# Two-layer sliding-window transformer on one core: row maxima that write two SBUF buffers in turn, and probability-times-value blocks ordered by key half

## The chip, the cores and the metric

The program runs on one core of one Trainium2 chip. The metric is the device time of the whole program in microseconds (us), the median of several runs. The names of the engines are those of the profile: PE (TensorE; PEld are its weight loads), DVE (VectorE), ACT (ScalarE), POOL (GpSimd) and SP (SyncE, which issues most DMAs).

## The reference

Two layers of attention (A) and feed-forward (B), with the same weights in both. 2048 rows of 640 numbers, 32 heads of 20, a causal window of 256 keys, a hidden width of 1536:

```python
scores = jnp.einsum("bhqd,bhkd->bhqk", q, k) * (Dh ** -0.5)
mask = (idx[:, None] - idx[None, :] >= 0) & (idx[:, None] - idx[None, :] < W)      # W = 256
scores = jnp.where(mask[None, None], scores, -1e9)
p = _softmax(scores, axis=-1)
o = jnp.einsum("bhqk,bhkd->bhqd", p, v)
...
x = x + _A_ref(_layernorm(x, axis=-1), A_wqkv, A_wo)
x = x + _B_ref(_layernorm(x, axis=-1), B_w1, B_b1, B_w2, B_b2)    # relu(h)^2 between w1 and w2
x = x + _A_ref(...)
x = x + _B_ref(...)
```

## The kernel before

The rows are cut into 16 **units** (8 groups of 256 rows in each of 2 layers, `u` = 0 to 15). A unit's attention is done in 8 **quads** of 4 heads. Because a row sees itself and 255 rows before it, a unit reads the keys of its own group (two blocks of 128, `kb` 2 and 3) and of the group before (`kb` 0 and 1). Units 0 and 8, the first groups of the layers, have only `kb` 2 and 3. That leaves 14 units, or 112 quads, with four blocks.

For one quad the work goes in five steps:

- `max_quad`: PE computes the scores once with queries on the partitions into `five`, five banks of PSUM (line 568; line 615 in units 0 and 8). DVE then takes the row maxima with eight `tensor_tensor_reduce` (`reduce`, line 578). Each adds a mask and writes the masked scores back over `five`, and is two instructions on DVE: the reduction (CUSTOM_DVE_ANT_0) and the read of its accumulator into `mx` (DVE_READ_ACCUMULATOR2_ANT).
- `max_out`: every second quad, the maxima are transposed (line 633), negated and sent by DMA into spare rows of `qt`, so that the next matmul subtracts them.
- `exp_quad`: PE computes the scores again with keys on the partitions, minus the maxima (line 684, line 693 in units 0, 1 and 8), into the same `five` and a further bank `sixth`. It has to wait until DVE has read the maxima out of `five`. ACT takes the exponentials into SBUF tiles `pt` (line 707). POOL sets what lies outside the window to zero (lines 722 and 726). Six exponentials and eight masks belong to a quad, in three steps: `kb` 1; `kb` 0 and 3; `kb` 2.
- `pv_quad`: PE multiplies by the values (line 765). The array is used as eight tiles of 64 rows by 32 columns: two **key halves** (`h`, the upper and the lower 64 keys of a block) times four heads. Half 0 sums in `pv`, half 1 in `sixth`. Since a half of an edge block sees only part of the queries, a block streams 256 and 192, or 128 and 64, columns in its two halves. The numbers are float32, so that each matmul shows as two records; a quad has 32 matmuls and 64 records here, and is called a **burst** below.
- ACT and DVE copy and add the two halves (lines 795 and 803), and DMA takes them away.

All the dense matmuls (projections and feed-forward, line 263, in float16 pairs) are poured between these steps by hand: `together` runs `exp_quad(n)`, some dense work, `max_quad` of a quad nine further on, `pv_quad(n)`, some dense work. The order on every engine is that in which the Python code emits it (a manual schedule). DVE, ACT and POOL jobs are queued with modelled costs and are emitted when the model says that they can start; `need` moves the model's clock on. `by_tiles` sorts the matmuls of a burst by where each would start in its own tile's stream, and `steps_of` lists the blocks of each step.

Of the kernel before, what the change touches and what calls it, by code (L numbers as in the profile page):

```python
# [12 lines left out]
BF16 = mybir.dt.bfloat16  # L13
AF = mybir.ActivationFunctionType
ALU = mybir.AluOpType

P = 128
Q = P // 2
# [27 lines left out]
def kernel(ctx: ExitStack, tc: tile.TileContext, x, wqkv, wo, w1, b1, w2, b2, out):  # L46
# [12 lines left out]
    maskb = sb.tile([P, 3 * P], BF16, name="maskb")  # L59
    nc.vector.memset(maskb, 0.0)  # L60

    nc.gpsimd.affine_select(out=maskb, in_=maskb, pattern=[[1, 3 * P]], compare_op=ALU.is_gt,
                            fill=NEG, base=0, channel_multiplier=-1)
    nc.gpsimd.affine_select(out=maskb, in_=maskb, pattern=[[-1, 3 * P]], compare_op=ALU.is_ge,
                            fill=NEG, base=2 * P, channel_multiplier=1)
    maskq = sb.tile([P, 5 * Q], BF16, name="maskq")
    b1s = sb.tile([P, FC], F32, name="b1s")
    kts = []
    for i in range(3):
# [469 lines left out]
    def by_tiles(pieces):  # L539
# [11 lines left out]
    maskj = []  # L551

    def max_pieces(n, e, w, x0, x1, m):

# [20 lines left out]

    def reduce(v, mask, accum, cols):

        bbjobs.append(post("D", 113 + 1.047 * cols, lambda: nc.vector.tensor_tensor_reduce(  # L578
            out=v, in0=v, in1=mask, scale=1.0, scalar=-3.0e38, op0=ALU.add, op1=ALU.max, accum_out=accum),
            prio=urgency["turn"]))  # L580

    def max_quad(n):

        u, qd = divmod(n, NQ)
        qt, cur = qts[u], kts[u % 3]
        G = qd // GQ
        if (u, G) not in mxs:
            mxs[u, G] = sb.tile([P, 2, 2 * GQ, 2], F32, name="mx", bufs=2)
        mx = mxs[u, G]
        need(trips[u, 0, qd], trips[u, 1, qd])  # L590
        banks()
        accum = {(e, w): mx[:, e, (2 * qd + w // 2) % (2 * GQ), w % 2:w % 2 + 1] for e in range(2) for w in range(4)}
        if u % NG:
            if not maskj:
                maskj.extend(post("D", 250, lambda h=h: nc.vector.tensor_copy(
                    maskq[h * Q:(h + 1) * Q, :], maskb[h * Q:(h + 1) * Q, h * Q:(h + 5) * Q]), prio=0) for h in range(2))
            need(*maskj)
            by_tiles([x for e in range(2) for w in TURN[e]
                      for x in max_pieces(n, e, w, LATER if w == 0 else 0, 5 * Q, Q)])
            now[0] += 656.0  # L600

            def rest():
                by_tiles([x for e in range(2) for x in max_pieces(n, e, 0, 0, LATER, P // 4)])
                now[0] += 110.0
# [5 lines left out]
            return  # L610
        for w in range(4):
            j, i = divmod(w, 2)
            for e in range(2):
                r, n_, o = slice(64 * e, 64 * e + 3 * DH), (i + 1) * P, i * P
                nc.tensor.matmul(five[:, 3 * e + j, o:o + n_], qt[r, 2 * qd + j, i * P:(i + 1) * P],
                                 cur[r, 2 * qd + j, :n_], start=True, stop=True)
        now[0] += 440.0
        for w in range(4):
            j, i = divmod(w, 2)
            for e in range(2):  # L620
                o, n_ = i * P, (i + 1) * P
                reduce(five[:, 3 * e + j, o:o + n_], maskb[:, 3 * P - n_:], accum[e, w], n_)
        mxjobs[u, G] = list(bbjobs)

    mxjobs = {}
# [109 lines left out]
    def steps_of(u):  # L735

        cur, prev = kts[u % 3], kts[(u - 1) % 3]
        if u % NG == 0:
            return [[(2, cur, 0, 0, 2)], [(3, cur, P, 1, 1)]]
        return [[(1, prev, P, 0, 2)], [(0, prev, 0, 0, 1), (3, cur, P, 1, 1)], [(2, cur, 0, 0, 2)]]  # L740

    def pv_quad(n, quad):
        u, qd = divmod(n, NQ)
        steps = steps_of(u)
        while rest_of:
            rest_of.pop()()
        pv, jobs = mm_tile([P, T], "pv")
        if u % NG:
            last_bank()
            two = (pv, sixth[:, :T])  # L750
            for k, pts in enumerate(quad[0]):
                need(*quad[1][k])
                pieces = []
                for kb, kt, ko, q0, qn in steps[k]:
                    vf = vts[(2 * (u if kb >= 2 else u - 1) + kb % 2) % 6][1]
                    for h in range(2):
                        a, b = seen(kb, h, qn * P)
                        for e, kb_, _, _, box, part in pts:
                            for j in range(2 if kb_ == kb else 0):
                                jj = 2 * j + e  # L760
                                c = (4 * qd + jj) * (DH + 1)

                                def put(h=h, kb=kb, jj=jj, c=c, j=j, vf=vf, box=box, part=part, a=a, b=b, q0=q0, k=k):
                                    pj = box["pt"][h * Q:(h + 1) * Q, part].rearrange("p (j n) -> p j n", j=2)
                                    nc.tensor.matmul(two[h][32 * jj:32 * (jj + 1), q0 * P + a:q0 * P + b],  # L765
                                                     vf[h * Q:(h + 1) * Q, c:c + 32], pj[:, j, a:b], start=(kb == 1),
                                                     stop=(k == len(steps) - 1), skip_group_check=True,
                                                     tile_position=(h * Q, 32 * jj))

                                pieces.append(((h, jj), b - a, put))  # L770
                by_tiles(pieces)
                now[0] += 410.0
        for k, pts in enumerate([] if u % NG else quad[0]):
            need(*quad[1][k])
            for kb, kt, ko, q0, qn in steps[k]:
                vf = vts[(2 * (u if kb >= 2 else u - 1) + kb % 2) % 6][1]
                for j in range(2):
                    for e, kb_, _, _, box, part in pts:
                        if kb_ == kb:
                            jj = 2 * j + e  # L780
                            c = (4 * qd + jj) * (DH + 1)
                            pj = box["pt"][:, part].rearrange("p (j n) -> p j n", j=2)
                            nc.tensor.matmul(pv[32 * jj:32 * (jj + 1), q0 * P:(q0 + qn) * P],
                                             vf[:, c:c + 32], pj[:, j, :], start=(k == 0),
                                             stop=(k == len(steps) - 1), skip_group_check=True,
                                             tile_position=(0, 32 * jj))
            now[0] += 480.0 if u % NG else 400.0
        if qd == 0:
            ods[u] = tc.dram_tile([DH + 1, H, T], F32, name=f"o{u}")
        if qd % 2 == 0:  # L790
            ots[u] = sb.tile([P, 2, T], F32, name="ot", bufs=2)
        ot = ots[u]

        def out():
            nc.scalar.copy(ot[:, qd % 2], pv)  # L795

        def write():
            drv = ods[u].rearrange("d (q j) n -> j d q n", j=4)
            for j in range(4):
                nc.sync.dma_start(drv[j][:, qd - 1:qd + 1, :], ot[32 * j:32 * j + DH + 1])  # L800

        def add():
            nc.vector.tensor_tensor(ot[:, qd % 2], ot[:, qd % 2], sixth[:, :T], op=ALU.add)  # L803
# [403 lines left out]
```

## Time and profile before

| | |
|---|---|
| median of 3 runs | 1659.91 us (1655.34 to 1662.32) |
| profiled execution: time | 1655.08 us |
| profiled execution: span of the trace | 1653.4 us |
| TensorE clock granted, mean | 0.994 |
| busy: PE, PEld | 1574.8 us (95%), 1209.9 us (73%) |
| busy: DVE, ACT, POOL | 1091.6 us (66%), 734.2 us (44%), 620.9 us (38%) |
| row maxima on DVE, 128 x 320 each (line 578) | 896 reductions, mean 497 ns |
| accumulator reads (line 578) | 1024, mean 141 ns |
| chain that ended last | PE 69%, DVE 18%, ACT 4% |

An instruction's row has its start, its length, its engine, its line in the kernel, what it writes and reads, and its shape; in brackets stands how long its engine was idle before it and what ended that. A matmul's length includes its way through the array, so that matmuls in a row overlap and only their starts tell the pace.

### The profile page before, as it was taken

What the parts mean: (1) busy time and instruction counts of PE and PEld (TensorE: products, weight loads), DVE (VectorE), ACT (ScalarE), POOL (GpSimd) and SP (SyncE); (2) the same over time, 40 slices, a digit from 0 to 9 for tenths busy, and PEclk for the clock granted to TensorE, in tenths of its full rate; (3) what the DMA queues carried; (4) which work ended last, traced back from release to release, by engine and by line L of the source; (5) the groups of instructions that cost most, each with busy time, mean ns of one, the idle gap of its engine ahead of it and who ended that gap; (6) DMA issues with size and microseconds to landing.
All of it is one profiled execution on the core that took longest, in us unless ns stands there. A gap on an engine that the chain in (4) does not pass through costs nothing.

```text
span 1653.4 us, 61438 instructions
## 1 busy us (share of the span) xinstructions
PE 1574.8 (95%) x25926; PEld 1209.9 (73%) x25926; DVE 1091.6 (66%) x3364; ACT 734.2 (44%) x1593; POOL 620.9 (38%) x1288
## 2 busy tenths in 40 slices
PE   8888999999999999999999999999999999998899
PEld 6666777777777777777777777777777777676667
DVE  8876766676757667576566767567675766857441
ACT  4454544445453444534443453534535444453422
POOL 1222534435342443524323352533534344353412
PEclk9999999999999999999999999999999999999999
DMA  9755244243433524343352435335253352421020
GB/s 267 186 138 138 51 111 93 64 124 67 118 79 98 122 51 117 82 119 85 86 130 56 113 86 122 79 93 110 62 120 86 102 102 59 105 67 54 27 64 17
DMA packets 234283, 159.16 MB, mean 96 GB/s; under 512 B 82200, under 2 KB 217752, under 8 KB 234008
## 3 DMA queue, kind: packets, MB, share of 16 engines
q1 hardware_dynamic: 227640, 145.74, 36.7%
q10 hardware_dynamic: 6368, 9.50, 2.0%
q8 instruction: 203, 3.33, 0.9%
q14 instruction: 72, 0.59, 0.1%
HBM read 84.68 MB, written 52.95 MB: 83 GB/s over the span
## 4 chain that ended last, share of the span: by engine, by line
PE 69%; DVE 18%; ACT 4%; issue 3%; POOL 3%; DMA 2%; SPq 0%; DVEq 0%; ACTq 0%; POOLq 0%
PE acc L263 51%; DVE five L578 10%; PE pv L765 5%; PE five L684 4%; PE five L568 4%; DVE mx L578 2%; ACT pt L707 2%; PE sixth L765 2%; POOL pt L726 2%; DVE hh L972 1%; DVE ot L803 1%; ACT r L962 1%; PE tr L633 1%; PE five L693 1%; DMA o<-ot 1%
## 5 line engine op out<-in xcount | busy, mean ns | idle before, releaser
L578 DVE CUSTOM_DVE_ANT_0 five<-five,maskq 128x320 f32<-128x320 f32 x896 | 445.6, 497 | 105.9 <-PE five L568 84.1
L707 ACT ACTIVATE pt<-five 128x512 f32<-128x512 f32 (+1 forms) x624 | 319.1, 595 | 267.5 <-PE sixth L684 216.3
L722 POOL TENSOR_SCALAR_AFFINE_SELECT pt<-pt 128x256 f32<-128x256 f32 x448 | 203.0, 462 | 545.6 <-ACT pt L707 528.1
L263 PE MATMUL acc<-y,w_s 128*128 128x256 f16 x2880 | 330.7, 273 | 5.3 <-ACT y L312 2.1
L263 PE MATMUL acc<-w_s,hh 128*128 128x320 f16 x2304 | 326.7, 299 | 0.0
L263 PEld LDWEIGHTS <-w_s 128*128 128x128 f16 x2880 | 277.9, 98 | 53.8 <-issue 19.4
L263 PEld LDWEIGHTS <-hh 128*128 128x128 f16 x2304 | 221.8, 98 | 94.2 <-issue 9.9
L726 POOL TENSOR_SCALAR_AFFINE_SELECT pt<-pt 128x256 f32<-128x256 f32 x512 | 227.5, 466 | 102.2 <-ACT pt L707 94.5
L263 PE MATMUL acc<-yT,wq_s 128*128 128x256 f16 x2250 | 260.0, 274 | 5.0 <-DVE qd L440 2.4
L263 PEld LDWEIGHTS <-wq_s 128*128 128x128 f16 x2400 | 231.4, 98 | 45.0 <-issue 12.9
L972 DVE TENSOR_TENSOR hh<-r,hh 128x256 f16<-128x256 f32 x192 | 90.9, 504 | 180.0 <-ACT hh L969 175.7
L966 POOL TENSOR_TENSOR r<-r 128x256 f32<-128x256 f32 x192 | 114.0, 614 | 185.6 <-ACT r L962 184.0
L765 PE MATMUL pv<-pt,vt 64*32 64x256 f32 (+3 forms) x3584 | 169.2, 301 | 5.1 <-DVE x L900 2.9
L765 PE MATMUL sixth<-pt,vt 64*32 64x192 f32 (+3 forms) x3584 | 159.7, 302 | 1.7 <-issue 1.7
L795 ACT COPY ot<-pv 128x256 f32<-128x256 f32 x128 | 47.6, 372 | 249.6 <-PE sixth L765 168.5
L263 PE MATMUL acc<-wo_s,od 128*128 128x320 f16 x960 | 141.1, 301 | 4.3 <-DVE od L876 2.9
L578 DVE DVE_READ_ACCUMULATOR2_ANT mx<- 128x1 f32 x1024 | 144.5, 141 | 0.0
L263 PE MATMUL acc<-wq_s,yT 128*128 128x320 f16 x900 | 134.1, 302 | 4.0 <-DVE y L313 2.8
L962 ACT ACTIVATE r<-acc,b1s 128x256 f32<-128x256 f32 x192 | 80.6, 471 | 107.9 <-PE acc L263 107.8
L263 PEld LDWEIGHTS <-od 128*128 128x128 f16 x960 | 91.6, 98 | 47.8 <-issue 5.0
L263 PEld LDWEIGHTS <-yT 128*128 128x128 f16 x900 | 87.2, 99 | 41.3 <-issue 9.9
L765 PEld LDWEIGHTS pv<-pt,vt 64*32 64x32 f32 x3584 | 101.3, 106 | 18.8 <-POOL pt L726 8.8
(96 smaller groups left out, 1617.4 us busy)
## 6 DMA issues: line engine op xcount, KB each, us to landing
qt<-qk SPq DMA_DIRECT2D x30, 480.0 KB
kt<-qk SPq DMA_DIRECT2D x30, 480.0 KB
qk<-qd SPq DMA_DIRECT2D x17, 640.0 KB
o<-ot SPq DMA_DIRECT2D x256, 42.0 KB
od<-o SPq DMA_DIRECT2D x14, 640.0 KB
qk<-yl SPq DMA_DIRECT2D x13, 640.0 KB
qk<-qd SPq DMA_DIRECT2D x17, 320.0 KB
xt<-in_A_x_dram SPq DMA_DIRECT2D x16, 320.0 KB
```

Source lines behind the costliest of these rows:

```text
L263: nc.tensor.matmul(acc, lhs(a, c), rhs(b, c), start=(k == 0), stop=(k == 3 * nk - 1))
L568: nc.tensor.matmul(flat[t * m:(t + 1) * m, o:o + b - a], qt[r, p, i * P + t * m:i * P + (t + 1) * m], kt[r, p, a + to:b + to], start=True, ...
L578: bbjobs.append(post("D", 113 + 1.047 * cols, lambda: nc.vector.tensor_tensor_reduce(out=v, in0=v, in1=mask, scale=1.0, scalar=-3.0e38, op ...
L684: nc.tensor.matmul(sbank[e][k][rows, o + a:o + b], kt[r, 2 * qd + j, ko + 64 * h:ko + 64 * (h + 1)], qt[r, 2 * qd + j, q0 * P + a:q0 * P + ...
L707: nc.scalar.activation(box["pt"][:, :o], sbank[e][k][:, :o], AF.Exp, scale=SCALE / (QS * QS))
L722: nc.gpsimd.affine_select(out=m, in_=m, pattern=[[0, 2], [-1, P]], compare_op=ALU.is_gt, fill=0.0, base=0, channel_multiplier=1)
L726: nc.gpsimd.affine_select(out=m, in_=m, pattern=[[0, 2], [1, P]], compare_op=ALU.is_ge, fill=0.0, base=0, channel_multiplier=-1)
L765: nc.tensor.matmul(two[h][32 * jj:32 * (jj + 1), q0 * P + a:q0 * P + b], vf[h * Q:(h + 1) * Q, c:c + 32], pj[:, j, a:b], start=(kb == 1), ...
L795: nc.scalar.copy(ot[:, qd % 2], pv)
L962: nc.scalar.activation(box["r"], acc[:, f, :], AF.Relu, bias=b1s[:, f0 + f:f0 + f + 1], scale=1.0 / (YS * WS))
L966: nc.gpsimd.tensor_tensor(box["r"], box["r"], box["r"], op=ALU.mult)
L972: nc.vector.tensor_sub(hh[:, 1, f, :], box["r"], hh[:, 0, f, :])
```

## The change

- The row maxima write their elementwise output (which nobody reads) to two bfloat16 buffers in SBUF, `junk0` and `junk1`, in turn, instead of back over `five`.
- The three steps of a quad are now `kb` 1; `kb` 2; `kb` 3 and 0. `pv_quad` takes the first two together and then the third, and each half goes through the blocks in an order of its own (`AFTER`), so that both halves stream 256, 192, 128, 64 columns, in that order. The first matmul of a sum (`start`) and the last (`stop`) follow this order.
- The masks of the maxima are packed: `maskq` alone, and a small `maskz`. They are built by POOL at the start, in place of two DVE copies made before their first use. So that they fit units 0 and 8 too, the scores there (line 615 before, 626 after) are computed in 64-query halves: 20 matmuls in a quad in place of 8.

```diff
+    masks = sb.tile([P, 3 * P], BF16, name="pt", tag="pt", bufs=6)
+    maskq = sb.tile([P, 5 * Q], BF16, name="maskq")
+    maskz = sb.tile([P, P], BF16, name="maskz")
...
+    nc.gpsimd.affine_select(out=maskz, in_=maskz, pattern=[[-1, P]], compare_op=ALU.is_ge,
+                            fill=NEG, base=0, channel_multiplier=1)
+    for h in range(2):
+        nc.gpsimd.tensor_copy(maskq[h * Q:(h + 1) * Q, :], masks[h * Q:(h + 1) * Q, h * Q:(h + 5) * Q])
...
+    junk, junked = [sb.tile([P, 5 * Q], BF16, name=f"junk{i}") for i in range(2)], []
...
     def reduce(v, mask, accum, cols):
-        bbjobs.append(post("D", 113 + 1.047 * cols, lambda: nc.vector.tensor_tensor_reduce(
-            out=v, in0=v, in1=mask, scale=1.0, scalar=-3.0e38, op0=ALU.add, op1=ALU.max, accum_out=accum),
-            prio=urgency["turn"]))
+        j = junk[len(junked) % 2]
+        junked.append(0)
+
+        def put():
+            nc.vector.tensor_tensor_reduce(out=j[:, :cols], in0=v, in1=mask, scale=1.0, scalar=-3.0e38,
+                                           op0=ALU.add, op1=ALU.max, accum_out=accum)
+
+        bbjobs.append(post("D", 113 + 1.047 * cols, put, prio=urgency["turn"]))
...
-            if not maskj:
-                maskj.extend(post("D", 250, lambda h=h: nc.vector.tensor_copy(
-                    maskq[h * Q:(h + 1) * Q, :], maskb[h * Q:(h + 1) * Q, h * Q:(h + 5) * Q]), prio=0) for h in range(2))
-            need(*maskj)
...
-                nc.tensor.matmul(five[:, 3 * e + j, o:o + n_], qt[r, 2 * qd + j, i * P:(i + 1) * P],
-                                 cur[r, 2 * qd + j, :n_], start=True, stop=True)
+                for h in range(2):
+                    for o, n_ in ([(0, P)] if i == 0 else [(P, 4 * Q)] if h else [(P, Q), (P + Q, 3 * Q)]):
+                        def put(e=e, r=r, p=p, h=h, i=i, j=j, o=o, n_=n_):
+                            nc.tensor.matmul(five[h * Q:(h + 1) * Q, 3 * e + j, o:o + n_], ...)
...
+    AFTER = ((2, 1, 3, 0), (1, 2, 0, 3))
...
-        return [[(1, prev, P, 0, 2)], [(0, prev, 0, 0, 1), (3, cur, P, 1, 1)], [(2, cur, 0, 0, 2)]]
+        return [[(1, prev, P, 0, 2)], [(2, cur, 0, 0, 2)], [(3, cur, P, 1, 1), (0, prev, 0, 0, 1)]]
...
-            for k, pts in enumerate(quad[0]):
-                need(*quad[1][k])
+            for ks, ns in (((0, 1), 830.0), ((2,), 400.0)):
+                need(*[j for k in ks for j in quad[1][k]])
...
-                    for h in range(2):
+                for h in range(2):
+                    for k, kb, kt, ko, q0, qn in sorted(blocks, key=lambda t: AFTER[h].index(t[1])):
...
-                                                     vf[h * Q:(h + 1) * Q, c:c + 32], pj[:, j, a:b], start=(kb == 1),
-                                                     stop=(k == len(steps) - 1), skip_group_check=True,
+                                                     vf[h * Q:(h + 1) * Q, c:c + 32], pj[:, j, a:b],
+                                                     start=(kb == 2 - h), stop=(kb == 3 * h), skip_group_check=True,
```

What this does to the order on two engines is shown here; the rows have the line, the operation and the tiles, and in brackets the engines whose semaphores an instruction waits for.

The first place is DVE, in a quad in the middle of a unit with four blocks. Before, three reductions with their accumulator reads and then the addition of the two halves (line 803) stand there:

```order
L578 ISA five,mx<-five,maskq 128x320 [waits PE_49]
L578 ISA mx 128x1
L578 ISA five,mx<-five,maskq 128x320 [waits DVE_49]
L578 ISA mx 128x1
L803 TENSOR_TENSOR ot<-ot,sixth 128x256 [waits DMAHW6_49,DMAHW0_49,DMAHW7_49,PE_49,Activation_49]
```

And after the change (the reduction is now on line 588):

```order
L588 ISA junk_135,mx<-five,maskq 128x320 [waits PE_49]
L588 ISA mx 128x1
L588 ISA junk_136,mx<-five,maskq 128x320
L588 ISA mx 128x1
L588 ISA junk_135,mx<-five,maskq 128x320 [waits DVE_49]
L588 ISA mx 128x1
L823 TENSOR_TENSOR ot<-ot,sixth 128x256 [waits DMAHW6_49,DMAHW0_49,DMAHW7_49,PE_49,Activation_49]
```

Nothing has changed its place. The second reduction waited for the first and waits for nothing now; the third still waits for DVE itself, because it writes the buffer that the one two places ahead wrote.

The second place is PE, one burst with the dense matmul behind it; `vt` with a number is the values of one block, `x4` are the four heads, and the last number is the columns streamed. Before:

```order
L765 MATMUL pv<-pt,vt_90 32x192 x4
L765 MATMUL sixth<-pt,vt_90 32x256 x4
L765 MATMUL pv<-pt,vt_87 32x64 x4
L765 MATMUL sixth<-pt,vt_87 32x128 x4
L765 MATMUL pv<-pt,vt_96 32x128 x4
L765 MATMUL sixth<-pt,vt_96 32x64 x4
L765 MATMUL pv<-pt,vt_93 32x256 x4
L765 MATMUL sixth<-pt,vt_93 32x192 x4
L263 MATMUL acc<-yT,wq_s 128x256
```

After (now on lines 785 and 269):

```order
L785 MATMUL pv<-pt,vt_100 32x256 x4
L785 MATMUL sixth<-pt,vt_97 32x256 x4
L785 MATMUL pv<-pt,vt_97 32x192 x4
L785 MATMUL sixth<-pt,vt_100 32x192 x4
L785 MATMUL pv<-pt,vt_103 32x128 x4
L785 MATMUL sixth<-pt,vt_94 32x128 x4
L785 MATMUL pv<-pt,vt_94 32x64 x4
L785 MATMUL sixth<-pt,vt_103 32x64 x4
L269 MATMUL acc<-yT,wq_s 128x256
```

The same 32 matmuls stand in the burst, 640 columns in each half; each pair of rows now has equal lengths. How much dense work stands between the steps on PE is the same in nearly all units.

More of the change, by code (lines that the diff above doesn't have):

```diff
@@ L620, in max_quad @@
             for e in range(2):
-                o, n_ = i * P, (i + 1) * P
-                reduce(five[:, 3 * e + j, o:o + n_], maskb[:, 3 * P - n_:], accum[e, w], n_)
+                if i:
+                    reduce(five[:, 3 * e + j, P:3 * P], maskq[:, Q:], accum[e, w], 2 * P)
+                else:
+                    reduce(five[:, 3 * e + j, :P], maskz, accum[e, w], P)
         mxjobs[u, G] = list(bbjobs)
@@ L750, in pv_quad @@
             two = (pv, sixth[:, :T])
-            for k, pts in enumerate(quad[0]):
-                need(*quad[1][k])
+            for ks, ns in (((0, 1), 830.0), ((2,), 400.0)):
+                need(*[j for k in ks for j in quad[1][k]])
+                blocks = [(k, *block) for k in ks for block in steps[k]]
                 pieces = []
-                for kb, kt, ko, q0, qn in steps[k]:
-                    vf = vts[(2 * (u if kb >= 2 else u - 1) + kb % 2) % 6][1]
-                    for h in range(2):
+                for h in range(2):
+                    for k, kb, kt, ko, q0, qn in sorted(blocks, key=lambda t: AFTER[h].index(t[1])):
                         a, b = seen(kb, h, qn * P)
-                        for e, kb_, _, _, box, part in pts:
+                        vf = vts[(2 * (u if kb >= 2 else u - 1) + kb % 2) % 6][1]
+                        for e, kb_, _, _, box, part in quad[0][k]:
                             for j in range(2 if kb_ == kb else 0):
```

22 lines of the change are left out of this document (13 added, 9 removed).

## The prediction

> **What bounds the kernel now.** I read the page first, then PE's waits in three stretches of the span, then the timelines of DVE and PE around one quad. The page's parts 1 and 4:
>
> ```profile
> PE 1574.8 (95%) x25926; PEld 1209.9 (73%) x25926; DVE 1091.6 (66%) x3364; ACT 734.2 (44%) x1593; POOL 620.9 (38%) x1288
> PE 69%; DVE 18%; ACT 4%; issue 3%; POOL 3%; DMA 2%; SPq 0%; DVEq 0%; ACTq 0%; POOLq 0%
> ```
>
> PE is idle for only 1653.4 − 1574.8 = 78.6 us. So time can be gained in two ways: PE waits less, or its own stream gets shorter. The chain nevertheless runs over DVE for 18%, so the idle time that there is should be DVE's doing. PE's waits (total, times, longest), first from 235 to 1420 us, then from 1420 to 1580 us, then from 0 to 235 us:
>
> ```profile
> PE five L684 <- DVE mx L578: 16.3, 23, 1.0
> ```
> ```profile
> PE five L684 <- DVE mx L578: 10.9, 10, 2.1
> PE acc L263 <- DVE od L876: 2.9, 2, 2.5
> ```
> ```profile
> PE five L693 <- DVE mx L578: 6.9, 9, 1.3
> PE pv L765 <- DVE x L900: 2.9, 1, 2.9
> PE acc L263 <- DVE y L313: 2.8, 2, 2.3
> PE five L684 <- DVE mx L578: 1.2, 1, 1.2
> ```
>
> PE wants to overwrite `five` with the second scores (684, 693) while DVE is still taking maxima out of it. That is 16.3 + 10.9 + 6.9 + 1.2 = 35.3 us in 43 waits. In the long middle no wait is over 1.0 us.
>
> **The reductions: how much earlier DVE is done.** DVE's timeline in the quad ahead of one such wait:
>
> ```profile
> 751.81 0.49 DVE L578 CUSTOM_DVE_ANT_0 five<-five,maskq 128x320 f32<-128x320 f32 x1
> ...
> 752.40 0.50 DVE L578 CUSTOM_DVE_ANT_0 five<-five,maskq 128x320 f32<-128x320 f32 x1
> ...
> 752.99 0.50 DVE L578 CUSTOM_DVE_ANT_0 five<-five,maskq 128x320 f32<-128x320 f32 x1
> ...
> 753.40 0.42 DVE L803 TENSOR_TENSOR ot<-ot,sixth 128x256 f32<-128x256 f32 x1
> ...
> 755.07 0.49 DVE L578 CUSTOM_DVE_ANT_0 five<-five,maskq 128x320 f32<-128x320 f32 x1
> ...
> 755.66 0.50 DVE L578 CUSTOM_DVE_ANT_0 five<-five,maskq 128x320 f32<-128x320 f32 x1
> ...
> 756.25 0.50 DVE L578 CUSTOM_DVE_ANT_0 five<-five,maskq 128x320 f32<-128x320 f32 x1
> ...
> 756.84 0.50 DVE L578 CUSTOM_DVE_ANT_0 five<-five,maskq 128x320 f32<-128x320 f32 x1
> ...
> 757.43 0.50 DVE L578 CUSTOM_DVE_ANT_0 five<-five,maskq 128x320 f32<-128x320 f32 x1
> ...
> 757.85 0.69 DVE L440 SCALAR_TENSOR_TENSOR yl<-acc,yl 128x512 f16<-128x512 f32 x1
> ```
>
> Start to start, a reduction that is followed by another takes 0.59 us (755.07 to 755.66, and so on). One that is followed by something else takes 0.41 (752.99 to 753.40) or 0.42 us (757.43 to 757.85). The length, 0.50 us, is the same. The difference is the wait in the order: the next reduction waits for the one before, while the addition and the line 440 do not. The accumulator read lies between in both cases and costs nothing in the second.
>
> With two buffers, the remaining wait is for the reduction two places ahead. That one started 2 × 0.415 = 0.83 us ago and took 0.50, so the wait is over before it is asked for. I therefore expect 0.415 us also between reductions, a gain of 0.175 us a pair. Not shown by this trace is a reduction started right behind an accumulator read without a wait, nor one that writes SBUF. The far bound is no gain at all (0.59). I take 0.415, since all the followers without a wait stand there, among them line 440, which reads PSUM and writes SBUF; a gain beyond it has no row. The quad above has six such pairs, so its last maximum comes 6 × 0.175 = 1.05 us earlier.
>
> A rule speaks against this: the Trainium skill, "VectorE: DVE Perf Modes", section "The DRAIN you can't avoid", says that after every operation the pipe has to run empty, and that eight copies took as long with a semaphore after each as with one at the end. By it this term would be nothing; the same section says that an operation that is not held starts earlier, and the trace, with 0.41 beside 0.59 us, sides with that half.
>
> **What that is worth on PE.** The wait behind this quad, and a place where PE goes from dense work to the second scores without one:
>
> ```profile
> 740.28 4.75 PE L263 MATMUL acc<-wo_s,od 128*128 128x320 f16 x33
> 744.96 0.63 PE L684 MATMUL five<-qt,kt 62*64 62x192 f16 x23
> ...
> 758.04 0.61 PE L684 MATMUL five<-qt,kt 62*64 62x192 f16 x23 [0.95 <-DVE mx L578]
> ```
>
> - 235 to 1420 us: the longest wait is 1.0 us and the quad comes 1.05 us earlier, so all 16.3 us go.
> - 1420 to 1580 us: ten waits, 1.09 us on average. Less dense work lies between the steps and other DVE work stands between the reductions, so I count 3 to 6 pairs ahead of each, 0.5 to 1.05 us. With what a wait has as its cap I take 7.8 of 10.9 us.
> - 0 to 235 us: ten waits, 8.1 us, nearly all shorter than 1.05 us. I take 7.6 us.
> - The other DVE waits (2.9 + 2.9 + 2.8 us) have 3 to 5 pairs ahead of them in DVE's queue, 0.5 to 0.9 us each; I take 3 us with the smaller ones.
> - Without a wait, PE starts the second scores 0.07 us before the modelled end of the dense matmul (744.96 against 740.28 + 4.75 = 745.03), with one it starts later by the whole idle time. So the waits that go, some 42, bring another 42 × 0.07 = 2.9 us.
>
> Together 16.3 + 7.8 + 7.6 + 3 + 2.9 = 37.6 us. What is late next at these places: nothing that the trace shows. The exponentials, masks and the burst follow the second scores at the same distance as before, and move forward with them.
>
> **The bursts.** PE's timeline of the burst in the same quad:
>
> ```profile
> 750.51 0.88 PE L568 MATMUL five<-kt,qt 60*64 60x64 f16 x45
> 751.21 0.34 PE L765 MATMUL pv<-pt,vt 64*32 64x192 f32 x4
> 751.23 0.39 PE L765 MATMUL sixth<-pt,vt 64*32 64x256 f32 x4
> 751.38 0.33 PE L765 MATMUL pv<-pt,vt 64*32 64x192 f32 x4
> 751.45 0.39 PE L765 MATMUL sixth<-pt,vt 64*32 64x256 f32 x4
> ...
> 752.19 0.41 PE L765 MATMUL pv<-pt,vt 64*32 64x256 f32 x3
> ...
> 752.55 4.54 PE L263 MATMUL acc<-yT,wq_s 128*128 128x256 f16 x40
> ```
>
> Each matmul goes through twice. 192 columns take 751.38 − 751.21 = 0.17 us and 256 take 0.22 us a pass, 0.86 ns a column. A half streams 640 columns twice: 640 × 2 × 0.86 ns = 1.10 us. The last pass of 256 starts at 752.19 and so ends at 752.41 to 752.45; the dense matmul starts 0.12 us later. The least that a burst can take is 1.10 + 0.12 = 1.22 us. It takes 752.55 − 751.21 = 1.34 us, because one half is ahead of the other and the array's weight loads come in order. With equal lengths side by side I expect 1.22 us, 0.12 us less. The bounds are 0 and 0.16 us. Busy time of line 765 in the whole span, and in this burst:
>
> ```profile
> 0.00:1654.00 1654.00, 171.07 (x7168) 122.37 (x7168) 0.99 0.40 96
> ```
> ```profile
> 751.00:753.00 2.00, 1.40 (x64) 1.07 (x64) 1.00 0.72 136
> ```
>
> 7168 / 64 = 112 bursts; the mean, 1.53 us, is not far above this one's 1.40, so most look like it. 112 × 0.12 = 13 us. The merged first group now waits for four masks where it waited for two; that is covered, as POOL shows for the same quad:
>
> ```profile
> 749.03 1.70 POOL L726 TENSOR_SCALAR_AFFINE_SELECT pt<-pt 128x256 f32<-128x256 f32 x3
> 750.71 0.54 POOL L300 TENSOR_TENSOR bmv<-bmv,neghalf 128x1 f32<-128x1 f32 x1
> ...
> 761.65 1.12 POOL L726 TENSOR_SCALAR_AFFINE_SELECT pt<-pt 128x256 f32<-128x256 f32 x3
> ```
>
> All eight masks end at 750.73, 0.48 us before the burst. The third group, which now has four masks in place of two, starts some 0.77 us (2 × 448 columns) into it, so its cover is 1.25 us. In bursts that do wait for the last mask, less work stands behind it than before.
>
> **Small edits.** In units 0 and 8 a quad's first scores are 20 matmuls in place of 8:
>
> ```profile
> 788.40 0.50 PE L615 MATMUL five<-kt,qt 60*128 60x128 f16 x8
> 788.84 0.37 PE L765 MATMUL pv<-pt,vt 64*32 64x192 f32 x4
> ```
>
> The eight take 0.44 us until the burst starts. The streams of the tiles keep their length, and in the row of 45 above a matmul costs 0.70 / 45 = 16 ns; 12 more are between 0 and 0.2 us a quad. For 16 quads I take 16 × 0.1 = 1.6 us. At the start POOL gets a selection and two copies, bounded by three times 0.51 us, ahead of the layernorm's power:
>
> ```profile
> 1.90 0.51 POOL L64 TENSOR_SCALAR_AFFINE_SELECT maskb<-maskb 128x384 bf16<-128x384 bf16 x1
> 5.49 0.55 POOL L300 TENSOR_TENSOR bmv<-bmv,neghalf 128x1 f32<-128x1 f32 x1 [3.09 <-DVE bmv L294]
> ```
>
> It was idle for 3.09 us there, so this costs nothing; without that cover, 1.5 us once.
>
> **The sum.** −37.6 (waits) − 13 (bursts) + 1.6 = −49 us, against the profiled execution's 1655.1 us: 1606.1 us. That execution was 4.8 us below the median of the three runs (1659.9), and as fast as the fastest of them. I take half of that, 2.4 us, as the median's distance: 1608.5 us, 3% less. A measurement of this kernel can tell about 0.5%, 8 us, from no change.
>
> **The rivals.**
> - *The reductions keep their pace.* The accumulator read has to end before the next reduction starts, or the remaining wait binds. Against it stand the 0.41 us followers; for it, that none of them is a reduction. All of the 37.6 us stay: 1608.5 + 37.6 = 1646 us.
> - *The bursts do not get shorter*, since weight loads and not unequal lengths make the 0.12 us. The reductions' part holds: 1608.5 + 13 = 1621.5 us.
> - *Slower: masks late behind reductions that write SBUF.* POOL's three masks took 1.70 us where a DVE operation from SBUF to SBUF ran beside them, and 1.12 us elsewhere (the two rows above), 0.58 us more. If reductions that write SBUF held POOL up like that, the four last masks of each burst would come later. It decides where they are over 1.25 us late, and from 0.44 us of waiting in each of the 112 bursts (49 us) the gain is gone. At 0.6 us each it is 112 × 0.6 = 67 us: 1608.5 + 67 = 1676 us. Against it: in this quad the masks end 1.1 us before the first reduction starts (750.73, 751.81), and a reduction reads a mask from SBUF already.
>
> **How the numbers follow.** Chances: forecast 0.74, unchanged bursts 0.09, unchanged reductions 0.09, late masks 0.08. The bound for faster lies near 1649 us, just above the 1646 us of the unchanged reductions, of which I count two thirds as faster. Faster 0.74 + 0.09 + 0.06 = 0.89, same 0.03, slower 0.08. The range: down to 1592, where the DVE waits left over (9 us) and bursts 0.16 us shorter (4.5 us) go too and the median lies at the profile; up to 1632, where half of the reductions' gain is missing (19 us) and the median lies 4.8 us above the profile. It takes in the unchanged bursts and leaves out the last two cases.
>
> **What would show it.** Right: reductions start every 0.41 to 0.42 us in a row; the waits of 684 and 693 (after: 703 and 712) for the maxima fall from 35 us to about 4; a clean burst takes some 1.22 us to the next dense matmul; PE's idle share falls to about 2.5%, with no new releaser among its waits. Wrong: starts 0.5 us or more apart; bursts that wait for POOL's masks; or PE waiting for ACT or a DMA at the second scores.

## The result, and the profile after

The changed kernel takes 1621.69 us (median of 5, 1619.97 to 1623.61) against 1658.33 us for the kernel before, measured beside it (5 runs). The ratio is 0.978, 95% interval 0.976 to 0.980: 2.2% less. The forecast was 1608.5 us with a range of 1592 to 1632 us; the time lies in it, 13 us above the forecast, where the rival "the bursts do not get shorter" had put it (1621.5 us).

The profiled execution took 1620.96 us (span 1618.9), 34.1 us less than that of before. First the busy row of the page:

```profile
PE 1568.2 (97%) x26118; PEld 1224.5 (76%) x26118; DVE 999.8 (62%) x3363; ACT 734.1 (45%) x1593; POOL 625.3 (39%) x1291
```

PE is idle for 1618.9 − 1568.2 = 50.7 us, where it was 78.6; its busy time fell by 6.6 us. PE's waits over the whole span (total, times, longest):

```profile
PE five L703 <- DVE mx L588: 6.7, 9, 1.4
PE five L574 <- ACT pt L726: 3.1, 5, 1.5
...
PE tr L650 <- DVE yl L446: 2.5, 12, 0.4
...
PE five L712 <- DVE mx L588: 0.6, 2, 0.4
```

The waits for the maxima have fallen from 35.3 us in 43 to 7.3 us in 11. None of them lies between 235 and 1390 us; in the same stretch of work before (235 to 1420 us) there had been 16.3 us. The third row is a wait that hardly showed before (0.4 us, once): the transpose of the maxima (line 650) comes 12 times some 0.2 us too early for DVE. PE's idle share is 3.1%, where the prediction named about 2.5%. DVE's timeline, three reductions in a row with their accumulator reads:

```profile
88.48 0.48 DVE L588 CUSTOM_DVE_ANT_0 junk<-five,maskq 128x320 bf16<-128x320 f32 x1
88.89 0.08 DVE L588 DVE_READ_ACCUMULATOR2_ANT mx<- 128x1 f32 x1
88.89 0.48 DVE L588 CUSTOM_DVE_ANT_0 junk<-five,maskq 128x320 bf16<-128x320 f32 x1
89.30 0.08 DVE L588 DVE_READ_ACCUMULATOR2_ANT mx<- 128x1 f32 x1
89.30 0.48 DVE L588 CUSTOM_DVE_ANT_0 junk<-five,maskq 128x320 bf16<-128x320 f32 x1
```

They start 0.41 us apart, where it was 0.59: the next one starts together with the read of the one before. The record of one is still 0.48 us long, so two overlap by 0.07 us.

The two DVE orders shown with the change differ by one reduction (two stand before the addition of the halves in the first, three in the second), so something did change its place: in 10 of the 112 quads a reduction has moved ahead of that addition. This comes from the new order of blocks, since the trace of the kernel before with that order alone has it too.

And a burst on PE, with what follows it:

```profile
740.98 0.39 PE L785 MATMUL pv<-pt,vt 64*32 64x256 f32 x4
740.99 0.39 PE L785 MATMUL sixth<-pt,vt 64*32 64x256 f32 x4
741.20 0.39 PE L785 MATMUL pv<-pt,vt 64*32 64x256 f32 x4
...
741.84 0.28 PE L785 MATMUL pv<-pt,vt 64*32 64x128 f32 x4
741.86 0.28 PE L785 MATMUL sixth<-pt,vt 64*32 64x128 f32 x4
741.95 0.25 PE L785 MATMUL pv<-pt,vt 64*32 64x64 f32 x4
742.01 0.24 PE L785 MATMUL sixth<-pt,vt 64*32 64x64 f32 x1
...
742.07 0.31 PE L785 MATMUL sixth<-pt,vt 64*32 64x64 f32 x6
742.31 0.45 PE L269 MATMUL acc<-wq_s,yT 128*128 128x320 f16 x2
```

The two halves run level down to the 128 columns, as intended, but the burst still takes 742.31 − 740.98 = 1.33 us. The last row of 128 columns starts at 741.86; at 0.86 ns a column its pass takes 0.11 us and two of 64 columns another 0.11 us, so the streaming would end at about 742.08. The dense matmul starts 0.23 us after that, not 0.12. Counted over all bursts that wait for nothing, from the first pass to the next dense matmul: 1.334 us before, 1.332 us after.

### The profile page after: what moved, and what is told of

The parts are those of the page before. It is cut to its first block, busy times and chain, and to the rows that moved or that the text cites. A ratio compares the mean times of both kernels' runs of the same rounds, so it can differ in the third digit from the quotient of the medians.

```text
span 1618.9 us, 61798 instructions
## 1 busy us (share of the span) xinstructions
PE 1568.2 (97%) x26118; PEld 1224.5 (76%) x26118; DVE 999.8 (62%) x3363; ACT 734.1 (45%) x1593; POOL 625.3 (39%) x1291
## 5 line engine op out<-in xcount | busy, mean ns | idle before, releaser
L588 DVE CUSTOM_DVE_ANT_0 junk<-five,maskq 128x320 bf16<-128x320 f32 (+1 forms) x960 | 411.4, 480 | 90.6 <-PE five L574 83.8
L992 DVE TENSOR_TENSOR hh<-r,hh 128x256 f16<-128x256 f32 x192 | 98.1, 532 | 205.1 <-ACT hh L989 196.7
L785 PE MATMUL sixth<-pt,vt 64*32 64x64 f32 (+3 forms) x3584 | 163.7, 299 | 2.7 <-POOL pt L741 0.9
L785 PE MATMUL pv<-pt,vt 64*32 64x64 f32 (+3 forms) x3584 | 151.5, 298 | 5.3 <-DVE x L920 2.4
L785 PEld LDWEIGHTS pv<-pt,vt 64*32 64x32 f32 x3584 | 107.2, 106 | 28.5 <-issue 4.1
L785 PEld LDWEIGHTS sixth<-pt,vt 64*32 64x32 f32 x3584 | 99.7, 105 | 8.6 <-POOL pt L741 7.7
```

What stands on the lines that cost most here:

```text
L588: nc.vector.tensor_tensor_reduce(out=j[:, :cols], in0=v, in1=mask, scale=1.0, scalar=-3.0e38, op0=ALU.add, op1=ALU.max, accum_out=accum)
L992: nc.vector.tensor_sub(hh[:, 1, f, :], box["r"], hh[:, 0, f, :])
```

## The experiments

Two questions were open: which of the edits brings the 34 us, and why the bursts did not get shorter. Where a ratio is given, the time is a median and stands beside runs of the kernel before on the same chip; where there is none, the kernel was run once. The first and last matmul of a sum (`start`, `stop`) follow the order of each run; those lines are not shown. "A clean burst" is counted in the trace as above, as the median of the bursts without a wait.

### Which edit brings the time

**The changed kernel with the old order of blocks.** Its edit puts back steps and groups (shown in part):

```diff
-        return [[(1, prev, P, 0, 2)], [(2, cur, 0, 0, 2)], [(3, cur, P, 1, 1), (0, prev, 0, 0, 1)]]
+        return [[(1, prev, P, 0, 2)], [(0, prev, 0, 0, 1), (3, cur, P, 1, 1)], [(2, cur, 0, 0, 2)]]
...
-            for ks, ns in (((0, 1), 830.0), ((2,), 400.0)):
-                need(*[j for k in ks for j in quad[1][k]])
+            for k, pts in enumerate(quad[0]):
+                need(*quad[1][k])
```

> The change without its second part: the steps of a quad and the block order of the bursts are those of before; the reductions still write two SBUF buffers. If the reductions' pace carries the whole gain, the time is within 4 us of the changed kernel (some 1620 us, ratio to before near 0.978), reductions stand 0.41 us apart and a clean burst takes 1.33 us. If the new block order carries a part, the time is 8 to 13 us higher (1630 us or more).

Measured: 1623.24 us, ratio 0.979 (0.977 to 0.980), reductions 0.41 us apart, a clean burst 1.333 us. Without the new order the gain is the same within the intervals.

**The kernel before with the new order of blocks alone** (the same lines the other way round):

> The kernel before with the second part alone: new steps and block order, reductions in place as before. If the block order is worth nothing, the time is that of before (within 4 us), reductions stay 0.59 us apart, the waits for the maxima stay near 35 us, and a clean burst takes 1.33 us in this order too. If it is worth what I forecast, 13 us less than before, bursts 1.22 us.

Measured: 1657.10 us, ratio 0.9985 (0.997 to 1.000), a clean burst 1.331 us. PE's waits:

```profile
PE five L686 <- DVE mx L578: 29.0, 34, 2.0
PE five L695 <- DVE mx L578: 5.9, 9, 1.3
```

They are those of before. The order of blocks is worth at most 5 us and perhaps nothing; the reductions bring the rest, together with the packed masks, which no run separates from them. What the order does give shows in the sum over all bursts, which holds their waits: 164.3 us here against 166.8 before.

**The changed kernel with one buffer in place of two.**

```diff
-    junk, junked = [sb.tile([P, 5 * Q], BF16, name=f"junk{i}") for i in range(2)], []
+    junk, junked = [sb.tile([P, 5 * Q], BF16, name=f"junk{i}") for i in range(1)], []
...
-        j = junk[len(junked) % 2]
+        j = junk[len(junked) % 1]
```

> The changed kernel with one SBUF buffer for the reductions in place of two, so that each reduction writes what the one just before it wrote and waits for it. If the wait made the pace, reductions go back to 0.58 or 0.59 us apart and the time to 1650 us or more. If the write to PSUM made it, they stay at 0.41 us and the time at 1621 us.

Measured: 1637.76 us, ratio 0.987 (0.986 to 0.989). DVE's timeline, and two of PE's waits:

```profile
90.98 0.49 DVE L588 CUSTOM_DVE_ANT_0 junk<-five,maskq 128x320 bf16<-128x320 f32 x1
91.40 0.08 DVE L588 DVE_READ_ACCUMULATOR2_ANT mx<- 128x1 f32 x1
91.52 0.49 DVE L588 CUSTOM_DVE_ANT_0 junk<-five,maskq 128x320 bf16<-128x320 f32 x1
```
```profile
PE five L703 <- DVE mx L588: 15.1, 22, 1.6
...
PE five L712 <- DVE mx L588: 2.8, 7, 0.8
```

With the wait for the reduction before, they start 0.54 us apart here and 0.53 in the median, neither 0.41 nor 0.59. So writing bf16 to SBUF in place of f32 to PSUM is worth 0.06 us a reduction even with the wait, and the wait itself 0.12 us. Place, type and writing over the own input changed together, and no run tells them apart. PE's waits for the maxima are 17.9 us here, between 35.3 and 7.3. In the kernel's time, all but the second buffer is worth 1658.8 − 1637.8 = 21 us (the order of blocks, at most 5 us, is in it), and the second buffer from there to 1621.7 (measured in another set) about 16 us. The second buffer is needed, and it is not the whole of it.

### Why the bursts kept their length

**Short blocks beside longer ones.** Half 0 ends with 64 and 128 columns, half 1 with 128 and 64:

```diff
-    AFTER = ((2, 1, 3, 0), (1, 2, 0, 3))
+    AFTER = ((2, 1, 0, 3), (1, 2, 0, 3))
```

> The changed kernel, where the last group of a burst has the 64-column blocks of one half beside the 128-column blocks of the other (half 0: 256, 192, 64, 128; half 1: 256, 192, 128, 64). If the burst loses its time at the end, where the 64-column blocks of both halves come together and their weight loads do not keep up, a clean burst falls from 1.33 to about 1.25 us and the time by 5 to 10 us. If a fixed cost of each of the 32 matmuls sets the burst, it stays at 1.33 us and the time at 1621 us.

Measured: 1624.99 us, ratio 0.980 (0.977 to 0.982), a clean burst 1.331 us. With uneven pairs at the end it takes as long as with even ones, and the time is not told apart from the changed kernel's. What changed is a wait:

```profile
PE pv L785 <- POOL pt L741: 8.5, 19, 0.8
```

Block 0's mask is the last one made, and is now needed earlier in half 0. In the changed kernel all waits of bursts for POOL are 2.7 us.

Four kernels then changed the number of matmuls and of columns. Three leave out part of the sum and the fourth adds it up wrongly, so they tell about time alone. **Shorter blocks, as many matmuls:**

```diff
                         a, b = seen(kb, h, qn * P)
+                        a, b = (a, (a + b) // 2) if (kb, h) not in ((2, 0), (1, 1)) else (a, b)
```

> The changed kernel with 448 in place of 640 columns in each half of a burst: all but the two 256-column blocks stream half their columns (96, 64, 32), so that part of P times V is left out. Still 32 matmuls in a burst. Theory A, PE can start only one pass every 20.8 ns on average (64 passes, 1.332 us), whatever their lengths: a clean burst stays at 1.33 us. Theory B, the columns set the time and the weight loads add a constant 0.23 us (1.33 - 1.10): 448 x 2 x 0.86 ns + 0.23 = 1.00 us. Theory C, every column is dearer than a long pass shows, 1.04 ns: 0.93 us. Whole kernel: A 1621 us, B about 37 us less.

Measured: 1.120 us a clean burst, 1610.24 us. None of the three is right: the burst got shorter, so there is no price of 20.8 ns on each pass, but not as short as its columns. PE's timeline:

```profile
740.89 0.25 PE L786 MATMUL pv<-pt,vt 64*32 64x96 f32 x4
...
740.98 0.25 PE L786 MATMUL pv<-pt,vt 64*32 64x96 f32 x4
...
741.06 0.30 PE L786 MATMUL pv<-pt,vt 64*32 64x64 f32 x5
...
741.58 0.58 PE L269 MATMUL acc<-wq_s,yT 128*128 128x320 f16 x3
```

The passes of 96 columns go on at their column price (0.08 to 0.09 us each). Then two of 64 and two of 32 columns, 0.16 us of streaming, take 0.52 us until the dense matmul. The loss sits in the short passes.

**Without the 64-column blocks:**

```diff
                         a, b = seen(kb, h, qn * P)
+                        if (kb, h) in ((0, 0), (3, 1)):
+                            continue
```

> The changed kernel without the eight 64-column matmuls of each burst (those blocks of P times V are left out): 24 matmuls, 576 columns in each half. Theory A (a price per pass): 48 x 20.8 ns = 1.00 us, or as long as the columns need if that is more, 576 x 2 x 0.86 ns = 0.99 us and 0.12 us for the last weight load, 1.11 us. Theory B (columns and a constant 0.23 us): 0.99 + 0.23 = 1.22 us. Theory C (1.04 ns a column): 1.20 us. Whole kernel: A about 1597 us, B and C about 1608 us.

Measured: 1.096 us, 1595.87 us. That is 576 × 2 × 0.86 ns = 0.99 us and 0.11 us, the sum under theory A for columns that bind. The two 64-column passes of a half thus cost 1.332 − 1.096 = 0.236 us, about as much as two of 128 columns (0.22 us).

**The same columns in 24 matmuls:**

```diff
                         a, b = seen(kb, h, qn * P)
+                        if (kb, h) in ((0, 0), (3, 1)):
+                            continue
+                        a, b = (a, b) if kb in (0, 3) else (0, qn * P)
```

> As the one before, 24 matmuls a burst, but the two 192-column blocks stream 256 columns, so that each half has 256, 256 and 128, the same 640 columns as the changed kernel (the 64-column blocks are left out, the added columns hold zeros). Theory A: the columns bound, 1.10 + 0.12 = 1.22 us, which is what the prediction took for 32 matmuls. Theories B and C: 1.33 us as before, since the columns are the same.

```profile
736.05 0.39 PE L788 MATMUL pv<-pt,vt 64*32 64x256 f32 x4
...
736.91 0.28 PE L788 MATMUL pv<-pt,vt 64*32 64x128 f32 x4
736.93 0.28 PE L788 MATMUL sixth<-pt,vt 64*32 64x128 f32 x4
737.02 0.28 PE L788 MATMUL pv<-pt,vt 64*32 64x128 f32 x4
737.04 0.28 PE L788 MATMUL sixth<-pt,vt 64*32 64x128 f32 x4
737.25 0.45 PE L269 MATMUL acc<-wq_s,yT 128*128 128x320 f16 x2
```

Measured: 1.203 us, 1608.34 us. With 640 columns in each half and no block shorter than 128, the burst takes what the prediction had worked out for it (1.22), and the kernel, which leaves out the 64-column blocks, is at the forecast time (by chance, since the waits fell short too, as told below). So 1.332 − 1.203 = 0.13 us of a burst is the price of the short passes, 112 × 0.13 = 14.5 us in the kernel, and equal pairs do not touch it.

**More matmuls, the same columns.** Each 256-column block is cut in two of 128. Both cuts carry the start flag, so the accumulated sums are not the reference's:

```diff
-                        a, b = seen(kb, h, qn * P)
+                        a0, b0 = seen(kb, h, qn * P)
...
+                        for a, b in ([(a0, a0 + P), (a0 + P, b0)] if (kb, h) in ((2, 0), (1, 1)) else [(a0, b0)]):
```

> The changed kernel with each 256-column matmul cut into two of 128: the same columns and the same result, 40 matmuls a burst in place of 32. Theory A: 80 passes x 20.8 ns = 1.66 us a burst, whole kernel some 112 x 0.33 = 37 us slower, about 1658 us. Theories B and C: 1.33 us, 1621 us.

Measured: 1.337 us, 1631.76 us. Eight more matmuls cost a clean burst 5 ns, so the number of passes alone is not the price either. Of the 11 us on the kernel (against the profiled 1620.96) the bursts explain little (their sum grew by 3.8 us); the rest includes longer idle times of PE that nothing in the profile ends:

```profile
PE acc L269 <- issue: 3.3, 3, 2.1
PE pv L786 <- issue: 3.0, 3, 1.7
```

All such rows make 9.4 us, where the changed kernel has 2.5.

In the tail of all these bursts the weight loads (PEld) of the short passes start mostly 12 to 17 ns apart. The loads of the changed kernel in the burst shown above:

```profile
741.74 0.12 PEld L785 LDWEIGHTS pv<-pt,vt 64*32 64x32 f32 x4
741.75 0.12 PEld L785 LDWEIGHTS sixth<-pt,vt 64*32 64x32 f32 x4
741.85 0.25 PEld L785 LDWEIGHTS pv<-pt,vt 64*32 64x32 f32 x8
742.00 0.21 PEld L785 LDWEIGHTS sixth<-pt,vt 64*32 64x32 f32 x8
```

The first two rows are a round: eight loads, both halves almost at once. In the last two, which are those of the short passes, half 1 gets its first load 0.15 us after half 0. After the first load of these sixteen (741.85) no other starts for 0.08 us, and the other fifteen start within 0.18 us, 13 ns apart on average. Eight loads, one round over the eight tiles, take about 0.13 us at 16.6 ns and 0.10 us at 13; 64 columns stream for 0.055 us. That suggested that loads come too slowly for short rounds, and two orders were tried that would hide this behind long rounds, if a lead could be built up.

**The short blocks first:**

```diff
-    AFTER = ((2, 1, 3, 0), (1, 2, 0, 3))
+    AFTER = ((0, 3, 1, 2), (3, 0, 1, 2))
...
-        return [[(1, prev, P, 0, 2)], [(2, cur, 0, 0, 2)], [(3, cur, P, 1, 1), (0, prev, 0, 0, 1)]]
+        return [[(3, cur, P, 1, 1), (0, prev, 0, 0, 1)], [(1, prev, P, 0, 2)], [(2, cur, 0, 0, 2)]]
```

> The changed kernel with the short blocks first: half 0 streams 64, 128, 192, 256 columns, half 1 64, 128, 256, 192; the step with blocks 3 and 0 is now the first of the three, so its exponentials and masks come first too. Same 32 matmuls, same result. Theory P (a round of eight passes cannot take less than 8 x 16.6 ns = 0.133 us, the pace of the weight loads at the end of the burst; a long round hides it, a 64-column round of 0.055 us does not, wherever it stands): a clean burst stays at 1.33 us, the kernel at 1622 us. Theory Q (loads are fetched ahead before the burst, and run dry only late in it, so that short rounds cost their surplus only at the end): the long rounds at the end hide the pace, a clean burst takes 1.20 us as the columns allow, 112 x 0.12 = 13 us less, 1609 us. In both POOL's masks of the third group are needed 0.7 us into the burst, as late as in the changed kernel, so no new waits.

Measured: 1620.63 us, ratio 0.978 (0.976 to 0.980), a clean burst 1.360 us.

```profile
744.48 0.23 PE L785 MATMUL sixth<-pt,vt 64*32 64x64 f32 x4
744.54 0.23 PE L785 MATMUL sixth<-pt,vt 64*32 64x64 f32 x4
744.69 0.29 PE L785 MATMUL sixth<-pt,vt 64*32 64x128 f32 x1
```

The short passes now run at some 0.055 us each, and the 128-column pass behind them, which could start at 744.60, comes 0.09 us late.

**The short blocks second:**

```diff
-    AFTER = ((2, 1, 3, 0), (1, 2, 0, 3))
+    AFTER = ((2, 0, 1, 3), (1, 3, 2, 0))
...
-            for ks, ns in (((0, 1), 830.0), ((2,), 400.0)):
+            for ks, at, ns in (((0, 1), (0,), 440.0), ((2,), (1, 2, 3), 790.0)):
```

> The changed kernel with the 64-column blocks second: both halves stream 256, 64, 192, 128 columns, level with each other. Same 32 matmuls, same result; the masks of blocks 3 and 0 are needed 0.44 us into the burst in place of 0.77. Theory P: a clean burst stays at 1.33 us. Theory Q: the surplus of the two 256-column rounds (2 x (0.22 - 0.133) = 0.17 us) covers the two short rounds (2 x (0.133 - 0.055) = 0.16 us), the 192-column rounds those of 128: 1.20 to 1.22 us. Masks that come too late cost some 8 us of PE waiting for POOL as in the run with a short beside a long block, so the kernel is at 1609 + 8 = 1617 us by Q and 1629 us by P.

Measured: 1637.55 us, ratio 0.988 (0.987 to 0.990), a clean burst 1.387 us, and

```profile
PE pv L785 <- POOL pt L741: 15.5, 25, 0.9
```

Here too the short passes run at 0.055 us and the next block starts late. Theory Q, a lead that long rounds build up, falls. Theory P has the sign, in that the loss goes with the short rounds wherever they stand, but both bursts are longer than its 1.33 us. And a strict 0.133 us a round would make the burst with halved blocks 0.44 + 6 × 0.133 + 0.10 = 1.34 us, where 1.12 was measured. At 0.10 us a round, the mean in the tail above, the same sum is 1.14 us, nearer to it; but the same loads keep up with the 96-column rounds of 0.08 us. What exactly paces the loads stays open.

**A way without the short blocks.** Blocks 0 and 3 over all 128 keys and all 128 queries, 24 matmuls with the full result:

```diff
-                        a, b = seen(kb, h, qn * P)
+                        if kb in (0, 3) and h:
+                            continue
+                        a, b = seen(kb, h, qn * P) if kb in (1, 2) else (0, P)
+                        rows = slice(h * Q, (h + 1) * Q) if kb in (1, 2) else slice(0, P)
```

> The changed kernel with blocks 0 and 3 taken over all 128 keys at once and all 128 queries (the masks have set the rest to zero), so that the 64-column matmuls are gone: 24 matmuls a burst, 256 and 192 columns in each half, then twice 128 columns over both halves, 704 columns in all against 640. Same result. If the 64-column rounds lose time because the next loads do not come fast enough: columns bound, 704 x 2 x 0.86 ns + 0.10 = 1.31 us against 1.33, the kernel some 2 us faster, about 1620 us. If a burst had a fixed price of its own beside its columns (0.23 us): 1.21 + 0.23 = 1.44 us, 12 us slower, 1634 us.

```profile
723.32 0.33 PE L788 MATMUL pv<-pt,vt 64*32 64x192 f32 x4
723.34 0.34 PE L788 MATMUL sixth<-pt,vt 64*32 64x192 f32 x4
723.60 0.64 PE L788 MATMUL pv<-pt,vt 128*32 128x128 f32 x16
724.18 0.31 PE L269 MATMUL acc<-wo_s,od 128*128 128x320 f16 x1
```

And the weight loads in the same burst:

```profile
723.18 0.12 PEld L788 LDWEIGHTS sixth<-pt,vt 64*32 64x32 f32 x4
723.60 0.27 PEld L788 LDWEIGHTS pv<-pt,vt 128*32 128x32 f32 x12 [0.30 <-issue]
```

Measured: 1630.19 us, ratio 0.983 (0.981 to 0.985), 1.451 us a clean burst. The value fits "a fixed price" (1.44), but the rows show another cause: the last 192-column passes start at 723.34 and stream 0.165 us, until 723.50; the first load for tiles of 128 rows starts at 723.60, 0.30 us after the load before it ended, where the 64-row loads run ahead of their passes. So by these rows no load runs ahead across the change from 64-row to 128-row tiles. Against the expectation's sum, which had left that change out, it costs 1.45 − 1.31 = 0.14 us.

**The same with these blocks first** (with the order of steps of the run with the short blocks first):

> As the one before, and the step with blocks 3 and 0 is the first of the three, as in the run with the short blocks first, where PE no longer waited for POOL's masks: the full-row matmuls come first, then 192 and 256 columns in half 0 and 256 and 192 in half 1. If the columns bind: 1.31 us a burst and 2 to 3 us less of waiting for masks, about 1617 us. If the halves being out of step costs as much as in the run with the short blocks first (1.36 there): 1.34 us, 1621 us.

```profile
669.80 0.43 PE L788 MATMUL pv<-pt,vt 128*32 128x128 f32 x8
670.16 0.64 PE L788 MATMUL sixth<-pt,vt 64*32 64x256 f32 x8
670.72 0.72 PE L788 MATMUL pv<-pt,vt 128*32 128x128 f32 x12
671.13 0.37 PE L788 MATMUL sixth<-pt,vt 64*32 64x192 f32 x4
```

Measured: 1711.08 us, ratio 1.031 (1.029 to 1.034), 2.17 us a burst. Half 1 begins in this order with its 256 columns between the two full blocks, so the tile changes from 128 to 64 rows and back, and the halves run one after the other while it does. At each of the three changes, in the median of the bursts, the first load of the new size starts 0.08 to 0.09 us after the last pass of the old one has streamed, as in the run before (0.09). A miss by 90 us: a mixture of tile sizes, which the expectation had not priced, costs more than anything the order of blocks could bring.

No kernel with the full result beats the changed one beyond the intervals.

## Why the prediction was right, and where it was not

**The reductions** were right to the hundredth: 0.41 us in a row as forecast, and the wait that is left does not bind. The reason given was only part of it. The prediction put the whole 0.175 us down to the wait; with the wait kept, writing bf16 to SBUF already gives 0.06 of it. For eight copies the Trainium skill, "VectorE: DVE Perf Modes", section "The DRAIN you can't avoid", reports that a semaphore after each cost nothing; that does not carry over to this operation, with 0.53 us with the wait and 0.41 without.

**The waits** were forecast at −37.6 us and came to about −32.2. That is a remainder, the 34.1 us less the bursts (−2.3) and the first scores (+0.4), and not all of it is waiting (see the clock below). Counted in the profile, PE's waits for DVE fell from 55.8 to 23.5 us, 28.0 of it for the maxima. The long middle gave all 16.3 us. From 1390 us on 5.0 us of maxima are left (3.1 were forecast), before 235 us 2.3 (0.5). "What is late next: nothing" was wrong by a little: 2.5 us at the transpose of the maxima, and PE's waits for ACT grew from 9.7 to 11.9 us in all.

**The clock** was a term that the prediction did not have. PE up to the first burst, before and after (busy time and matmuls, granted clock):

```profile
0.00:137.20 137.20, 115.56 (x1206) 0.96 0.76 205
0.00:127.00 127.00, 112.11 (x1298) 1.00 0.81 216
```

For the same work, and 92 matmuls more, PE was busy 3.4 us less at the higher clock. Over the whole spans, 1653 × (1 − 0.994) − 1619 × (1 − 0.996) = 3.4 us is an estimate of what the clock took off the 34.1 us. It is no accident of two executions: beside the experiments there are 30 runs of the kernel before, at 0.990 to 0.994, and five of the changed one at 0.995 or 0.996. Within one kernel the time follows it too: the four runs of the kernel with short blocks beside longer ones took 1620.95 us at 0.997, 1623.23 at 0.996, 1626.75 at 0.995 and 1629.43 at 0.992. The changed kernel with the old order of blocks was at 0.995 or 0.996 and the kernel before with the new order at 0.990 to 0.992 in nine of ten runs, so the higher clock goes with the reductions; how it comes about no run shows.

**The bursts** are the step that failed: −13 us forecast, 166.8 to 164.5 us in all 112, so −2.3 us, and not from clean bursts. The sum "a half streams 640 columns twice, 1.10 us, and 0.12 us" holds for blocks of 128 columns and more (1.203 and 1.096 us). For 32 matmuls with two short passes in each tile's chain it does not, and the reason given, "one half is ahead of the other", was not the cause: the burst took 1.331 to 1.334 us in the order of before, in that of after and with uneven ends, and more in two others. The rival with unchanged bursts named weight loads; the runs tie the loss to the short passes, and the pace of loads behind it is a reading of the trace, not shown apart. At 0.09 that rival was rated too low: the one burst shown in the prediction had a wrongly explained 0.12 us, and no row with level halves and short blocks. That the median meets this rival's 1621.5 us to 0.2 us is luck: it had all of the forecast waits going, and the 2.4 us that were put between profile and median turned out to be 0.7.

**The small edits**: the 20 first-score matmuls take 0.461 us in place of 0.435, 0.4 us in 16 quads, not 1.6. The merged groups' cover nearly held: bursts wait for POOL's masks 2.7 us in six places, where it was 0.2 us in one.

**The slower rival**: the masks that lay for more than half of their time beside reductions took 0.51 us on average (28 of them), and 0.52 us before (26), so reductions that write SBUF hold the masks up no more than those that wrote PSUM.

The sum: bursts 10.7 us short, waits 5.4 short, first scores 1.2 better: 14.9 us, the whole distance from −49 to −34.1. It closes because the waits are taken as the remainder; without the clock's 3.4 us they are some 9 us short. The upper end of the range holds a slip: with the median 4.8 us above the profile it is 1606.1 + 19 + 4.8 = 1630 us, not 1632. The measured time lies below both.

## What to carry to other kernels

An operation whose elementwise output nobody reads still makes its successor wait where both write the same tile (before the change each reduction wrote columns of `five` of its own, and the order has the wait all the same): give it two buffers in turn, and ask where and in what type it writes, since that and the wait are two separate prices. A length worked out from the streaming price of long blocks is a lower bound for bursts that hold short ones, not their time; one run with as many columns in longer blocks shows which it is. Before short blocks are rearranged, look for what the new order needs: of those tried, two made PE wait for masks, two paid for changes of the tile size, and none gained by pairing. And compare the granted clock of the two kernels before a difference in time is put down to the edit's own terms.

## What was not expected of the hardware

- A reduction from PSUM that writes bf16 to SBUF and waits for the one before starts every 0.53 us, one that writes f32 back to PSUM every 0.59 us; without the wait 0.41 us, with records of 0.48 us that overlap.
- Two passes of 64 columns in each of eight tiles cost 0.236 us at the end of a burst, about what two of 128 stream (0.22 us), where the streaming of the 64 alone is 0.11 us.
- Going from 64-row to 128-row tiles within a burst cost 0.14 us against the sum by columns: the first load of the new size starts only 0.09 us after the streaming has ended. A burst that goes back and forth took 2.17 us in place of 1.33.
